# Token-major queries and keys of two chunks by DMA transpose instead of TensorE and ScalarE, in a one-core transformer-layer backward kernel

## The chip, the cores and the metric

The kernel runs on one core of a Trainium2 chip. The metric is the device time of one execution in microseconds; for a kernel it is the median of several runs. The kernel before takes 562.0 us (three runs, 561.25 to 563.71).

## What is computed

One pre-layernorm transformer layer, forward and backward: 2048 tokens of width 512 (D), 32 heads of 16, a sliding and dilated attention (each query sees 8 keys, at distances 0, 2, ... 14), then a GELU feed-forward of width 1792. The outputs are the layer's result and the gradients of the input, of the four weight matrices and of the two biases. Everything is bf16.

```python
def _A_ref(x, wqkv, wo):
    qkv = (x @ wqkv).reshape(B, S, 3, H, Dh)...      # q, k, v per head
    idx = pos[:, None] - (arange(8) * 2)[None, :]    # 8 dilated keys, masked below 0
    logits = einsum("bhsd,bhswd->bhsw", q, k[idx]) * Dh ** -0.5
    o = einsum("bhsw,bhswd->bhsd", softmax(logits), v[idx])
    return o.reshape(B, S, D) @ wo
def _B_ref(x, w1, b1, w2, b2):
    return gelu(x @ w1 + b1) @ w2 + b2
h  = x + _A_ref(layernorm(x), wqkv, wo)
h2 = h + _B_ref(layernorm(h), w1, b1, w2, b2)        # and jax.vjp of all of it with grad_out
```

## The kernel before

**Stages.** The tokens are cut into four chunks (c = 0 to 3) of 512. Per chunk there is an attention forward (`p1_ln`, `p1_qkv`, `p1_attn`, `p1_o`, `p1_h`), the feed-forward with its backward (`p2_h`, `p2_out`, `p2_dg`, `p2_bwd`), and the attention backward (`p3_go`, `p3_dots`, `p3_bands`, `p3_gl1`). At the end come the weight gradients (`wg_ffn`). These are not run one after another: the whole program is a list of about 2000 small operations (`op(...)`), each with an engine, and two tables written out at the end of the file say in which order they are emitted (`ORDER`) and at which SBUF address or PSUM bank each buffer lies (`HOMES`). Every engine works through its own share of that order and stops at the first operation whose inputs or whose buffer are not ready. So an operation that stalls on an engine holds up all that stands behind it there, the DMA issues of SyncE (SP) and of GpSimd (POOL) included.

**Projections.** `p1_proj` multiplies the layernormed chunk by the q or k columns of `wqk` (line 570) and ScalarE evicts the result to `qt` or `kt`, feature-major: features on the partitions, tokens along the row. `kt` has 16 more columns in front (`PAD`), the last tokens of the chunk before; `p1_qkv` copies them from that chunk's `kt` (line 602). `dots` multiplies on VectorE (DVE) four times per chunk: query block times the eight shifted key blocks, one product `prf` of 128 x 4096 (line 428), and TensorE sums it over the features of a head (line 436) with a matrix of ones and zeros, `Emat` or `S32`.

**Token-major copies.** The backward's `gather` reads queries, keys and values back from DRAM token by token (`q_d`, `k_d`, `v_d`), with the features in the order "position in the head, then head". `to_tm_store` makes that copy for q and k: per chunk and tensor two groups of eight 128 x 128 transposes on TensorE (line 393), in which the matrix `Pmat` also reorders the features, one ScalarE eviction per group (line 276, tiles `tmq`, `tmk`) and one store of 256 KB per group on the SP queue (line 266).

**The other way, already in the file.** `tm_dma` does the same by DMA transposes issued from SP (`xload`, line 270) into a tile `tm..d`, and one store of 512 KB. It can't reorder features. In the kernel before only the attention output gradient (`go`, all chunks, tile `tmgod`) goes this way. `TMD` lists who does. `QKP` lists the chunks whose q and k are projected with `wqp`, a copy of `wqk` with its columns already in "position, head" order; it is empty before, and then neither `wqp` nor the copies that fill it exist.

**GpSimd.** POOL computes the layernorm's rstd for chunks 1 to 3 (line 343), issues the gathers (line 418), and makes one reordered weight copy, `woT` from `woR` (line 1066), of the same form and size as each of the two copies that would fill `wqp`.

Of the kernel before, what the change touches and what calls it, by code (L numbers as in the profile page):

```python
# [10 lines left out]
P = 128  # L11
# [9 lines left out]
PAD = 16  # L21
# [127 lines left out]
def kernel(  # L149
# [26 lines left out]
    S, D = xf.shape  # L176
    F = B_w1.shape[1]
    NT = S // P
    CH = 512
# [413 lines left out]
    def p1_qkv(c):  # L593
# [5 lines left out]
        else:  # L599
            kp = st_[c - 1]["kt"]  # L600
            if (c in QKP) == (c - 1 in QKP):
                op("DVE", 0.12, lambda: V.tensor_copy(out=kt()[:, :, 0:PAD], in_=kp()[:, :, CH:CH + PAD]), r=[(kp, 0), (kp, 1)], w=[(kt, "h")], tag="halo")
            else:
                ps = ps_("psh")
                lp = st_[c - 1]["ln1T"]

                def hm():
                    for g in range(4):
                        for dc in range(DC):
                            T.matmul(ps()[:, g * PAD:(g + 1) * PAD], lhsT=wqp()[:, dc, D + g * P:D + (g + 1) * P], rhs=lp()[:, dc, CH - PAD:CH],  # L610
                                     start=(dc == 0), stop=(dc == DC - 1))
                op("PE", 1.0, hm, r=[(wqp, 1), lp], w=[ps], tag="khalo", cls=0)
                op("DVE", 0.15, lambda: V.tensor_copy(out=kt()[:, :, 0:PAD], in_=ps()[:, 0:4 * PAD].rearrange("p (g n) -> p g n", g=4)), r=[ps], w=[(kt, "h")], tag="halo")
# [509 lines left out]
QKP = ()  # L1123
TMD = (('go', 0), ('go', 1), ('go', 2), ('go', 3))
# [162 lines left out]
```

## Time and profile before

| | before |
|---|---|
| median of 3 runs | 562.0 us (561.25 to 563.71) |
| profiled execution, its own time | 562.08 us |
| its span, first to last instruction | 560.3 us |
| TensorE (PE) busy | 538.7 us (96%) |
| VectorE (DVE) busy | 496.2 us (89%) |
| ScalarE (ACT) busy | 314.8 us (56%) |
| mean granted TensorE clock | 0.999 |

The profile is one execution. Busy is the time in which an engine had an instruction running; a matmul's end is modelled, so a busy PE is not yet a PE at its peak. "PEld" is the load of the stationary operand, which overlaps the matmuls. The DMA share is the mean busy share of the core's 16 DMA engines. An idle gap is put down to what ended it. Tiles are shown without their numbers, and a line can be that of a helper: line 276 is every plain eviction, line 270 every DMA transpose.

### The profile page before, as it was taken

The page shows a single profiled execution, that of the slowest core. Times are in us where ns is not written, and L with a number is a line of the kernel's source. Part 1 is how long each engine was busy: PE and PEld are TensorE (multiplying, and loading weights), DVE is VectorE, ACT ScalarE, POOL GpSimd, SP SyncE. Part 2 cuts the span into 40 slices and gives each one's busy share as a digit, 9 for nine tenths or more (in the row PEclk, how much of TensorE's full clock was granted, in tenths as well). Part 3 has the DMA queues.
Part 4 walks back from the last instruction along what each step waited for, and adds up shares of the span by engine and source line. Part 5 has one row for each costly group of instructions (what it writes and reads, how often), then busy time and mean ns, then how long its engine had stood idle before and what let it go on. Part 6 is the DMA issues. An engine that isn't in the chain of part 4 may idle for free. (4 is left out here: it accounts for less than half of the span.)

```text
span 560.3 us, 8579 instructions
## 1 busy us (share of the span) xinstructions
PE 538.7 (96%) x3281; PEld 247.9 (44%) x3330; DVE 496.2 (89%) x651; ACT 314.8 (56%) x498; POOL 36.2 (6%) x55
## 2 busy tenths in 40 slices
PE   7799989999999999999999999999999999999996
PEld 3344444344444444444444444464444444444442
DVE  7989999999999999899886287798999898999944
ACT  4887589997989965885411224222235526543432
POOL 0210011020000100002000000000010110100000
PEclk9999999999999999999999999999999999999999
DMA  8898979999297383479789999999989999887773
GB/s 248 230 286 241 324 247 308 271 236 259 90 242 202 121 188 84 123 151 256 157 151 186 199 207 152 251 211 232 242 272 322 364 274 364 320 332 180 230 190 96
DMA packets 199673, 126.65 MB, mean 226 GB/s; under 512 B 152080, under 2 KB 193232, under 8 KB 195536
## 3 DMA queue, kind: packets, MB, share of 16 engines
q1 hardware_dynamic: 194016, 84.68, 64.3%
q0 software_dynamic: 5616, 41.42, 19.8%
q8 instruction: 26, 0.43, 0.3%
q14 instruction: 15, 0.12, 0.1%
HBM read 55.74 MB, written 35.21 MB: 162 GB/s over the span
## 5 line engine op out<-in xcount | busy, mean ns | idle before, releaser
L276 ACT CAST wgs<-ps 128x512 bf16<-128x512 f32 (+1 forms) x30 | 16.3, 557 | 69.4 <-PE ps L940 61.2
L794 PE MATMUL ps<-goT,w2T 128*128 128x512 bf16 x224 | 54.3, 379 | 0.5 <-DVE h2s L768 0.5
L712 PE MATMUL ps<-ln2T,w 128*128 128x512 bf16 x224 | 53.3, 379 | 0.1
L808 PE MATMUL ps<-w1T,xb 128*128 128x512 bf16 x218 | 51.5, 379 | 0.4
L766 PE MATMUL ps<-w,gl 128*128 128x512 bf16 x219 | 51.2, 379 | 0.6 <-DVE h2s L768 0.3
L714 ACT ACTIVATE xb<-ps,b1c 128x512 bf16<-128x512 f32 x56 | 36.4, 691 | 19.3 <-PE ps L712 19.2
L914 PE MATMUL ps<-wqkvT,gqkvT 128*128 128x512 bf16 x183 | 44.3, 379 | 0.5 <-issue 0.2
L796 DVE SCALAR_TENSOR_TENSOR xb<-xb,ps 128x512 bf16<-128x512 bf16 x56 | 36.7, 681 | 8.7 <-PE ps L794 8.2
L428 DVE TENSOR_TENSOR prb<-got,vw 128x4096 bf16<-128x4096 bf16 x16 | 36.1, 2285 | 8.2 <-ACT got L276 7.0
L940 PE MATMUL ps<-gw1in,ln 128*128 128x512 bf16 (+1 forms) x185 | 38.6, 351 | 0.8 <-issue 0.6
L940 PE MATMUL ps<-gor,gw2in 128*128 128x512 bf16 x164 | 38.8, 379 | 0.2
L467 DVE TENSOR_TENSOR prbv<-Rv,cfv 128x4096 bf16<-128x4096 bf16 x16 | 35.7, 2284 | 2.0 <-DMA Rv<-go_d 1.7
L467 DVE TENSOR_TENSOR prbk<-Rk,cfk 128x4096 bf16<-128x4096 bf16 x16 | 35.9, 2286 | 1.4 <-PE ps L476 1.3
L467 DVE TENSOR_TENSOR prbq<-Rq,cfq 128x4096 bf16<-128x4096 bf16 x16 | 35.9, 2285 | 1.3 <-DMA Rq<-k_d 1.0
L467 DVE TENSOR_TENSOR prbo<-Ro,cfo 128x4096 bf16<-128x4096 bf16 x16 | 35.7, 2281 | 0.0
L428 DVE TENSOR_TENSOR prf<-qt,kt 128x4096 bf16<-128x4096 bf16 x16 | 35.7, 2285 | 0.0
L940 PEld LDWEIGHTS <-ln 128*128 128x128 bf16 x256 | 24.3, 98 | 24.4 <-issue 3.0
L794 PEld LDWEIGHTS <-w2T 128*128 128x128 bf16 x224 | 21.8, 98 | 27.2 <-issue 1.6
L766 PEld LDWEIGHTS <-gl 128*128 128x128 bf16 x224 | 21.7, 98 | 27.2 <-issue 1.1
L808 PEld LDWEIGHTS <-xb 128*128 128x128 bf16 x224 | 21.9, 98 | 26.4
L712 PEld LDWEIGHTS <-w 128*128 128x128 bf16 x224 | 21.3, 98 | 26.2 <-issue 2.1
L570 PE MATMUL ps<-ln1T,wqk 128*128 128x512 bf16 x127 | 30.2, 379 | 2.0 <-DMA wqk<-in_A_wqkv_dram 1.9
(173 smaller groups left out, 964.7 us busy)
## 6 DMA issues: line engine op xcount, KB each, us to landing
Ro<-v_d POOLq DMA_DIRECT2D x4, 1280.0 KB, 9.0
Rq<-k_d POOLq DMA_DIRECT2D x4, 1280.0 KB, 8.5
Rv<-go_d POOLq DMA_DIRECT2D x4, 1280.0 KB, 8.7
Rk<-q_d POOLq DMA_DIRECT2D x4, 1280.0 KB, 6.6
g_d<-gl SPq DMA_DIRECT2D x9, 512.0 KB, 3.8
gh_d<-xb SPq DMA_DIRECT2D x9, 512.0 KB, 3.4
Ro<-v_d POOLq DMA_DIRECT2D x4, 1024.0 KB, 6.3
Rq<-k_d POOLq DMA_DIRECT2D x4, 1024.0 KB, 9.8
```

What stands on the lines that cost most here:

```text
L276: fn = lambda: A.copy(out=ap(), in_=pap())
L428: op("DVE", tt_us(4096), lambda g=g, pr=pr: V.tensor_tensor(out=pr(), in0=ql()[:, g, :].unsqueeze(1).to_broadcast([P, W, 512]), in1=_sub(k ...
L467: V.tensor_tensor(out=pr().rearrange("p a j (d h) -> p a j d h", h=H), in0=_sub(R()[:, o0, 0:1], [[st, 2], [512, 4], [32, DH], [1, H]]), i ...
L570: T.matmul(ps()[:, gg * 512:(gg + 1) * 512], lhsT=wq_()[:, dc, sel * D + g * P:sel * D + (g + 1) * P], rhs=cols(st_[c]["ln1T"], dc, c in F ...
L712: T.matmul(ps(), lhsT=w1()[:, dc, f * P:(f + 1) * P], rhs=cols(ln2T[c], dc, c in FM2), start=(dc == 0), stop=(dc == DC - 1))
L714: op("ACT", act_us(512, 1), lambda f=f, ps=ps, xb=xb, f0=f0: A.activation(out=xb()[:, f - f0, :], in_=ps(), func=ACT.Identity, bias=b1c[:, ...
L766: T.matmul(ps(), lhsT=d["g"][f // 4]()[:, f % 4, j * P:(j + 1) * P], rhs=w2()[:, f, :], start=(f == 0), stop=(f == FT - 1))
L794: T.matmul(ps(), lhsT=w2T()[:, dc, f * P:(f + 1) * P], rhs=cols(goT, dc, True), start=(dc == 0), stop=(dc == DC - 1))
L796: op("DVE", 0.61, lambda f=f, ps=ps, z=z, f0=f0: V.scalar_tensor_tensor(out=z()[:, f - f0, :], in0=z()[:, f - f0, :], scalar=1.0, in1=ps() ...
L808: T.matmul(ps(), lhsT=d["d"][f // 4]()[:, f % 4, j * P:(j + 1) * P], rhs=w1T()[:, f, :], start=(f == 0), stop=(f == FT - 1))
L914: T.matmul(ps(), lhsT=gT()[:, j, b * P:(b + 1) * P], rhs=wqkvT()[:, k0 + b, :], start=(i == 0 and b == 0), stop=(i == 2 and b == 3))
L940: T.matmul(ps()[:, 0:N], lhsT=l, rhs=r, start=(n == 0), stop=(n == k - 1))
```

## The change

`QKP` becomes (2, 3): the queries and keys of chunks 2 and 3 are projected with `wqp`. `TMD` gets q and k of chunks 2 and 3: their token-major copies go through `tm_dma`. What follows from these two settings in code that stands in the file already:

- POOL fills `wqp` in two copies (keys, then queries), each of 2048 elements per partition, from `wqk`. In the new order both stand on POOL behind the rstd of chunk 2 and ahead of that of chunk 3 and of the first gathers of `Ro`.
- Chunk 2's `kt` can't take its 16 front columns from chunk 1's `kt`, whose features lie in another order. They are computed again from chunk 1's `ln1T`: 16 matmuls of 16 columns (`khalo`) and a small DVE copy. The one changed line of code gives the right slice of `ln1T` where that tile is laid out by the DMA transpose (`FM1`).
- `dots` sums the products of chunks 2 and 3 with `S32` instead of `Emat`, in matmuls of the same shape.
- For each of the four (tensor, chunk) pairs, 16 TensorE transposes, two evictions and two stores go; for a query chunk one DMA transpose of 512 KB and a store in 256-byte pieces come, for a key chunk four DMA transposes of 128 KB and a store.

`ORDER` and `HOMES` are new throughout (1982 operations instead of 1989, 869 buffers instead of 879).

```diff
                         for dc in range(DC):
-                            T.matmul(ps()[:, g * PAD:(g + 1) * PAD], lhsT=wqp()[:, dc, D + g * P:D + (g + 1) * P], rhs=lp()[:, dc, CH - PAD:CH],
+                            T.matmul(ps()[:, g * PAD:(g + 1) * PAD], lhsT=wqp()[:, dc, D + g * P:D + (g + 1) * P], rhs=lp()[:, TPC - 1, (dc + 1) * P - PAD:(dc + 1) * P] if c - 1 in FM1 else lp()[:, dc, CH - PAD:CH],
                                      start=(dc == 0), stop=(dc == DC - 1))
...
-QKP = ()
-TMD = (('go', 0), ('go', 1), ('go', 2), ('go', 3))
+QKP = (2, 3)
+TMD = (('go', 0), ('go', 1), ('go', 2), ('go', 3), ('q', 2), ('k', 2), ('q', 3), ('k', 3))
...
 ORDER = (
-    9, 6, 12, 7, 19, 0, 4, 21, 22, 1, 70, 3, 25, 37, 5, 8, 18, 10, 20, 11, 2, 51, 47, 52,
...
```

The code that the settings switch on:

```python
for i in (1, 0) if QKP else ():
    op("POOL", 3.9, lambda i=i: G.tensor_copy(out=wqp()[:, :, i * D:(i + 1) * D].rearrange("p a (d h) -> p a d h", h=H),
                                              in_=_sub(wqk()[:, 0, 0:1], [[2 * D, DC], [1, DH], [DH, H]], i * D)), r=[(wqk, i)], w=[(wqp, i)], tag="hinwq")
...
def tm_dma(fm, off, dst, c, back, tag, pm):
    st = sb("tm" + tag + "d", [P, 4, 512])
    r = c * CH + (RPAD if back else 0)
    if off:
        for g in range(4):
            xload(st, lambda g=g: st()[:, :, g * P:(g + 1) * P], lambda g=g: fm()[:, g, off:off + CH], 128, r=[(fm, g // 2)], key=g, tag="tmx" + tag)
        store(dst, lambda: dst()[r:r + CH, :].rearrange("(a p) d -> p a d", p=P), st, lambda: st(), 512, key=(c, 0), tag="tmst" + tag)
    else:
        xload(st, ..., lambda: fm().rearrange("p g t -> p (g t)"), 512, r=[(fm, 0), (fm, 1)], tag="tmx" + tag)
        store(dst, ..., row=0.25)
```

239 rows, old and new, of tables (HOMES, ORDER) are left out of this document.

## The prediction

> **What bounds the kernel now.** I read the busy totals first, then the table of twenty-microsecond stretches, then who waited for whom inside the stretch that the change touches.
>
> ```profile
> span 560.3 us, 8579 instructions
> PE 538.7 (96%) x3281; PEld 247.9 (44%) x3330; DVE 496.2 (89%) x651; ACT 314.8 (56%) x498; POOL 36.2 (6%) x55
> ...
> 20.00:40.00 20.00, 18.18 (x136) 8.92 (x136) 17.97 (x25) 18.01 (x22) 2.75 (x4) 1.00 0.90 256
> 40.00:60.00 20.00, 19.45 (x145) 8.74 (x146) 20.00 (x10) 14.43 (x20) 0.00 (x0) 1.00 0.85 242
> 60.00:80.00 20.00, 18.96 (x165) 9.84 (x165) 19.86 (x27) 13.50 (x16) 3.04 (x4) 1.00 0.82 297
> 80.00:100.00 20.00, 18.17 (x155) 8.57 (x156) 20.00 (x12) 19.48 (x31) 1.61 (x3) 1.00 0.97 298
> 100.00:120.00 20.00, 19.73 (x128) 8.28 (x128) 19.79 (x32) 19.93 (x24) 1.76 (x2) 1.00 0.94 248
> 120.00:140.00 20.00, 20.00 (x94) 9.00 (x93) 19.39 (x35) 15.59 (x22) 2.15 (x3) 1.00 0.95 252
> 140.00:160.00 20.00, 20.00 (x122) 8.89 (x121) 19.80 (x22) 19.54 (x27) 0.54 (x1) 1.00 0.54 121
> ```
>
> The columns of the stretches are PE, PEld, DVE, ACT and POOL busy, the granted clock, the DMA share and GB/s. Over the whole span PE is the bound: 538.7 of 560.3 us. But the change sits in the attention forward, roughly 20 to 120 us, and there the reading is another. From 40 to 120 DVE is idle for 0.35 us in all (0 + 0.14 + 0 + 0.21), PE for 3.7 (0.55 + 1.04 + 1.83 + 0.27). In that stage VectorE leads and TensorE follows; from 120 on PE is full and has work queued. Who ended the idle time says the same. PE's waits, 20 to 120:
>
> ```profile
> PE ps L393 <- ACT tmv L276: 1.2, 1, 1.2
> PE ps L634 <- DVE mx L629: 1.1, 3, 0.6
> PE ps L436 <- DVE prf L428: 1.1, 1, 1.1
> PE ps L476 <- ACT tmv L276: 0.7, 1, 0.7
> PE ps L393 <- ACT kt L276: 0.2, 1, 0.2
> ```
>
> and DVE's, 20 to 140:
>
> ```profile
> DVE rtr L1053 <- POOL rstd L343: 1.1, 1, 1.1
> DVE r L647 <- PE ps L642: 0.6, 1, 0.6
> DVE h2s L768 <- PE ps L766: 0.4, 1, 0.4
> ```
>
> So two prices matter: what PE and ACT are spared, and what DVE is charged. A microsecond lost on DVE before about 120 us delays the products that PE then sums; a microsecond saved on PE there counts only as far as PE, not DVE, was late.
>
> **What TensorE and ScalarE are spared.**
>
> ```profile
> L393 PE MATMUL ps<-Pmat,qt 128*128 128x128 bf16 x64 | 4.9, 219 | 2.7 <-ACT qt L276 1.6 <-ACT tmv L276 1.2
> L393 PE MATMUL ps<-Pmat,kt 128*128 128x128 bf16 x64 | 4.9, 219 | 0.2 <-ACT kt L276 0.2
> L276 ACT COPY tmk<-ps 128x1024 bf16<-128x1024 bf16 x8 | 8.2, 1024 | 1.1 <-PE ps L393 1.1
> L276 ACT COPY tmq<-ps 128x1024 bf16<-128x1024 bf16 x8 | 8.1, 1029 | 0.1
> ...
> 38.40 0.61 PE L393 MATMUL ps<-Pmat,kt 128*128 128x128 bf16 x8
> 38.85 1.89 PE L570 MATMUL ps<-ln1T,wqk 128*128 128x512 bf16 x8
> ```
>
> Half of the 128 transposes go: 8 groups of 8. A group's pitch is what it delays the next matmul by, 38.85 - 38.40 = 0.45 us (the mean of 219 ns overlaps), so 8 x 0.45 = 3.6 us of PE. The khalo matmuls come back: 16, each with its own weight load and 16 columns. The nearest row is the transpose, 0.45 / 8 = 0.056 us with its weight load and 128 columns; an eighth of that, 0.007, is the other end, so 0.1 to 0.9 us. I take 0.9, since each has a whole weight load. Net 2.7 us of PE. The summing matmuls keep their shape: nothing. ACT loses 8 evictions of 1.03, 8.2 us, in a stage where it is 97 to 100% busy from 80 to 120; PE's waits for ACT above (1.2 + 0.7 + 0.2 = 2.1 us) could shrink.
>
> What is it worth to the end? At most 2.7 + 2.1 = 4.8 us, at least nothing, since PE may spend it waiting for DVE. The new order uses the freed slots for feed-forward matmuls, but these hang on DVE's layernorm statistics too. I take 1.3 us, half of the net PE time: DVE has only 0.35 us of idle time to give up in this stage, yet some of the matmuls that move up don't wait for it.
>
> **What VectorE is charged.** The costly addition is not the transposes but the two POOL copies that fill `wqp`. The trace has their twin, `woT`:
>
> ```profile
> L1066 POOL COPY woT<-woR 128x2048 bf16<-128x2048 bf16 x1 | 3.9, 3888 | 69.6 <-DMA gh_d<-xb 69.6
> ...
> 255.27 3.89 POOL L1066 COPY woT<-woR 128x2048 bf16<-128x2048 bf16 x1 [69.63 <-DMA gh_d<-xb]
> ...
> 134.59 0.69 DVE L733 TENSOR_SCALAR ga<-x 128x2048 bf16<-128x2048 bf16 x1
> ...
> 255.62 4.09 DVE L733 TENSOR_SCALAR ga<-x 128x2048 bf16<-128x2048 bf16 x1
> ...
> 17.38 2.28 DVE L428 TENSOR_TENSOR prf<-qt,kt 128x4096 bf16<-128x4096 bf16 x1
> ...
> 17.47 3.06 POOL L343 TENSOR_TENSOR rstd<-ve,mhalf 128x4 f32<-128x4 f32 x1 [0.76 <-DVE nm L346]
> 31.39 1.01 POOL L343 TENSOR_TENSOR rstd<-ve,mhalf 128x4 f32<-128x4 f32 x1 [10.86 <-DVE ve L341]
> ```
>
> Two readings. At 255.27 the copy starts on POOL, and the DVE instruction that starts at 255.62 takes 4.09 us instead of 0.69: it ends at 259.71, which is the copy's end at 259.16 plus about its own length. DVE stood still while POOL copied. The other way round, POOL's rstd, 1.01 us alone, took 3.06 when it started 0.09 us after a product: it ended 0.87 us after the product did. So DVE and POOL exclude each other here, and the one that came first is not interrupted. The Trainium skill states this as a rule, in SBUF — State Buffer, section "Who interferes with whom": VectorE and GpSimd share a pair of ports, whichever issues first holds it for the whole instruction, and an instruction with two SBUF inputs, as a product is, contends with a GpSimd instruction that reads SBUF. Both rows agree; by that rule alone the copies could also be the ones that wait, which is the first rival.
>
> Where do the copies fall? Ahead of them on POOL stand only the rstd of chunks 1 and 2, and their input `wqk` is in use by the first projections. So they start right behind the rstd of chunk 2, beside the first chunk's four products.
>
> ```profile
> 21.94 4.48 DVE L428 TENSOR_TENSOR prf<-qt,kt 128x4096 bf16<-128x4096 bf16 x2
> ...
> 32.43 0.21 DVE L1053 STREAM_TRANSPOSE rtr<-rstd 128x32 f32<-128x32 f32 x1 [1.12 <-POOL rstd L343]
> ```
>
> In the new order the rstd of chunk 2 is released behind the first product, so it runs when the second ends, near 22 us, and the first copy asks for SBUF during the third product. It gets in behind that, since a small DVE instruction (nm of chunk 2) stands between the third and the fourth, and the fourth then waits 3.9 us less some 0.1. The second copy finds the fourth product waiting or running, lets it pass, and runs in the stretch after it that has no products: from 26.42 (the end of the row above) to 32.43 DVE does statistics and a maximum, 6.0 us without a product, more than the 3.9 needed. So one copy is charged, 3.8 us, with 0 and 7.8 (2 x 3.89) as ends; a gain is excluded, since copies only add. Behind the copies on POOL wait the rstd of chunk 3 and the first gathers. DVE's wait for that rstd, 1.12 us at 32.43, goes: the new order puts the instructions that need it behind the softmax of chunk 0. And the gathers have all four products of chunk 1 for cover, as the new order puts these ahead of the first band product. DVE's net loss is 3.8 - 1.1 = 2.7 us.
>
> **What SP and the DMA engines are charged.**
>
> ```profile
> q_d<-tmq SPq DMA_DIRECT2D x8, 256.0 KB, 3.3
> k_d<-tmk SPq DMA_DIRECT2D x8, 256.0 KB, 3.8
> go_d<-tmgod SPq DMA_DIRECT2D x4, 512.0 KB, 4.4
> tmgod<-got SPq DMA_TRANSPOSE x4, 4.5
> ...
> L270 SPq DMA_TRANSPOSE tmgod<-got x4: 1866/2914/3837, 327.3 to 453.3; - x4
> ...
> 109.46 3.65 SPq L270 DMA_TRANSPOSE w2T<-in_B_w_dram  x2
> ...
> 126.62 1.03 PE L794 MATMUL ps<-goT,w2T 128*128 128x512 bf16 x4
> ```
>
> The stores carry the same bytes in half as many pieces: about nothing. The transposes of 4 x 512 KB are new. One holds the SP queue for 2.9 us at the median, so 4 x 2.9 = 11.7 us of queue, and I take the same for the DMA engines. By their place in the new order they run between about 55 and 150 us. From 60 to 140 the DMA share leaves 20 x (0.18 + 0.03 + 0.06 + 0.05) = 6.4 us, and the next stretch 9.2 more. Nobody needs the copies before the backward's gathers. What stands behind them on SP is wanted, but early: the last of `w2T` was issued by 113.1, landed some 4.5 us later, and was first used at 126.62, 9 us of slack. So I put this at nothing; what it costs if that cover is gone is the third rival.
>
> **Sum.** 562.08 (the profiled execution, its span plus 1.8; the median of the runs is 562.0, so no shift) - 1.3 + 2.7 = 563.5 us. About 0.5%, 2.8 us, is what a measurement of this kernel can tell from no change; this sum lies inside it.
>
> **Rivals.** First, the copies cost DVE nothing: they come late enough, or lose every race, as the rstd did at 17.47. Then PE's relief shows: 562.1 - 2.7 - 1.1 (the wait that goes), 558.3, and down to 556.2 if ACT's 2.1 go too. For it: an order that was planned with such stalls would put the copies where DVE does statistics. Against it: nothing holds POOL until then. Second, slower: both copies go ahead of a product. The second follows the first on POOL at once, before the blocked product is through: 7.8 - 1.1 - 1.3, 567.5 us. It decides where POOL keeps the port between two of its instructions; no row shows that. Third, slower as well, the transposes crowd the DMA: of their 11.7 us 5.3 don't fit before 140, and if the order has put so much of it ahead of `w2T` that this slips beyond its 9 us, PE waits: 563.5 + 5.3 = 568.8. Against it: 9 us is more than 5.3. The Trainium skill speaks for it, in VectorE: DVE Perf Modes, section "The three transpose paths": a 128 x 128 transpose is given as 390 ns on TensorE and 1309 by DMA, and the advice is TensorE where PSUM will do. By an estimate from that page 64 tiles would take 59 us more. The trace agrees in direction only: 0.056 us on PE, 4.5 / 16 = 0.28 by DMA.
>
> **How the numbers follow.** My forecast has 0.42, and its own range is 561 to 566; of it 0.36 lies within 0.5% of before (559.2 to 564.8) and 0.06 above. The first rival has 0.30: 0.24 below 559.2, 0.06 within. The second has 0.18 and the third 0.10, of which 0.26 lie above 564.8 and 0.02 within. Faster 0.24, same 0.44, slower 0.32. The range 557 to 570 leaves out some 0.08 below (ACT's whole relief) and 0.10 above (two slow cases together). As all of the order is new, each case also carries its luck, some microseconds either way.
>
> **What would show it.** One product of chunk 0 of about 6 us instead of 2.28, beside a POOL copy at 22 to 30 us; the other copy beside statistics. PE's idle time from 40 to 120 grown from 3.7 us to 5 or 6, ended by DVE, and none by ACT's `tmv`. DMA share from 80 to 160 higher, with no PE wait on DMA. PE busy 536 in total. I am wrong if all products last 2.28 (first rival), two are long (second), or a wait on `w2T` or `ln2T` appears (third); and if these hold but the time doesn't, the order past 160 us did it.

## The result and the profile after

The changed kernel took 566.9 us, median of 4 runs (566.01 to 567.8), against 561.9 of the kernel before (561.25 to 563.71, 4 runs): a ratio of 1.0084, 95% interval 1.0055 to 1.0112. It is slower by 0.84%. That lies inside the forecast range of 557 to 570, but above the 563.5 that was forecast, above that forecast's own range of 561 to 566, and outside the likeliest class, no change. The number of the prediction that comes nearest is the second rival's 567.5; its mechanism is not what the profiled execution shows. That execution took 566.01 us, the fastest of the four.

The page after, its span and its busy totals; then the stretches of twenty microseconds, with the columns of before:

```profile
span 564.2 us, 8539 instructions
...
PE 542.3 (96%) x3282; PEld 245.0 (43%) x3282; DVE 499.0 (88%) x651; ACT 308.1 (55%) x490; POOL 47.5 (8%) x57
```
```profile
20.00:40.00 20.00, 16.23 (x141) 8.13 (x139) 18.02 (x24) 16.02 (x20) 14.79 (x6) 0.91 0.67 177
40.00:60.00 20.00, 19.23 (x133) 7.24 (x130) 20.00 (x11) 12.28 (x15) 0.00 (x0) 1.00 1.07 303
60.00:80.00 20.00, 18.10 (x139) 8.69 (x139) 19.86 (x27) 11.15 (x14) 2.68 (x4) 1.00 0.94 296
80.00:100.00 20.00, 17.84 (x141) 7.68 (x139) 20.00 (x13) 15.47 (x25) 1.59 (x3) 1.00 0.87 251
100.00:120.00 20.00, 18.50 (x128) 8.24 (x126) 19.83 (x27) 19.39 (x23) 1.61 (x2) 1.00 1.15 279
120.00:140.00 20.00, 19.93 (x94) 8.92 (x92) 19.86 (x38) 17.80 (x24) 1.03 (x1) 1.00 0.91 220
140.00:160.00 20.00, 18.08 (x102) 7.86 (x101) 16.62 (x18) 16.15 (x24) 1.48 (x2) 1.00 0.79 255
```

ScalarE's 314.8 us became 308.1: 6.7 of the 8.2 us that the eight evictions were put at. TensorE's total can't be compared: the trace of before holds 3330 weight loads but 3281 matmuls, so 49 records of matmuls are missing there. The first stretch has what matters: TensorE 16.2 us busy instead of 18.2 and a granted clock of 0.91. And a later stretch that was full before, 140 to 160, now has VectorE idle for 3.4 us and TensorE for 1.9.

VectorE's timeline in the first stretch (start, duration), and POOL's:

```profile
20.53 2.28 DVE L428 TENSOR_TENSOR prf<-qt,kt 128x4096 bf16<-128x4096 bf16 x1
22.73 3.88 DVE L346 SCALAR_TENSOR_TENSOR nm<-mv,rstd 128x4 f32<-128x4 f32 x1
26.53 2.28 DVE L428 TENSOR_TENSOR prf<-qt,kt 128x4096 bf16<-128x4096 bf16 x1
28.73 0.68 DVE L330 BATCH_NORM_STATS2 st<-xt 128x6 f32<-128x512 bf16 x1
...
36.54 0.69 DVE L649 TENSOR_TENSOR attn<-e,r 128x1024 bf16<-128x1024 bf16 x1
```
```profile
21.36 11.21 POOL L1010 COPY wqp<-wqk 128x2048 bf16<-128x2048 bf16 x2
```

The copies asked for SBUF at 21.36, the third product held it until 22.73, then the first copy ran; it was the tiny `nm` (128 x 4) that stood still, 3.88 us instead of 0.15, with the fourth product queued behind it. The second copy lost to that product and ran beside the statistics, which kept their 0.68 us. TensorE, in the same place, and its clock in two stretches of 2 us:

```profile
28.86 1.04 PE L436 MATMUL ps<-prf,Emat 128*32 128x512 bf16 x8 [3.76 <-DVE prf L428]
29.84 2.94 PE L570 MATMUL ps<-ln1T,wqk 128*128 128x512 bf16 x8
```
```profile
28.00:30.00 2.00, 1.14 (x9) 0.26 (x9) 1.64 (x4) 2.00 (x4) 2.00 (x1) 0.64 0.86 293
30.00:32.00 2.00, 2.00 (x6) 0.66 (x5) 1.97 (x3) 1.81 (x3) 2.00 (x1) 0.51 0.11 37
```

It waited 3.76 us for the product and came back at about half its clock: eight projection matmuls took 2.94 us, where the same eight take 1.89 a little later.

The difference can be cut into legs with four marks that every trace has: the start of the first product (`prf`), the start of the first attention instruction (`attn<-e,r`), the end of the last band product (`prbo`), and the end of the last matmul. In us, each from the mark before:

| kernel | first product | to attention | to last band product | to last matmul |
|---|---|---|---|---|
| before | 17.38 | 16.96 | 118.53 | 402.55 |
| after | 15.97 | 20.57 | 124.02 | 398.21 |

The last two columns belong together, since the new order moves work across the mark: 521.08 before, 522.23 after. So the change of 3.9 us in span (560.3 to 564.2) is -1.41 before the first product, +3.61 from there to attention, +1.15 from attention to the last matmul, and +0.55 in the tail behind it.

### The profile page after: what moved, and what is told of

The parts are those of the page before. It is cut to its first block, busy times and chain, and to the rows that moved or that the text cites. A ratio compares the mean times of both kernels' runs of the same rounds, so it can differ in the third digit from the quotient of the medians.

```text
span 564.2 us, 8539 instructions
## 1 busy us (share of the span) xinstructions
PE 542.3 (96%) x3282; PEld 245.0 (43%) x3282; DVE 499.0 (88%) x651; ACT 308.1 (55%) x490; POOL 47.5 (8%) x57
## 3 DMA queue, kind: packets, MB, share of 16 engines
q1 hardware_dynamic: 205536, 86.78, 66.5%
## 4 chain that ended last, share of the span: by engine, by line
PE 75%; DVE 16%; DMA 3%; ACT 3%; issue 2%; SPq 0%; POOL 0%; DVEq 0%; POOLq 0%; ACTq 0%
PE ps L940 27%; PE ps L808 9%; PE ps L914 7%; PE ps L794 7%; PE ps L766 6%; DVE prf L428 5%; PE ps L476 4%; PE ps L712 2%; PE ps L832 2%; PE ps L570 2%; DVE prbo L467 2%; PE ps L436 2%; DVE st L330 2%; DMA xp<-in_A_x_dram 1%; PE ps L492 1%
## 5 line engine op out<-in xcount | busy, mean ns | idle before, releaser
L712 PE MATMUL ps<-ln2T,w 128*128 128x512 bf16 x224 | 52.0, 379 | 1.5 <-DMA ln2T<-ln 1.4
L940 PE MATMUL ps<-gor,gw2in 128*128 128x512 bf16 x168 | 40.0, 379 | 0.0
L940 PE MATMUL ps<-gw1in,ln 128*128 128x512 bf16 (+1 forms) x192 | 40.0, 353 | 0.0
L736 ACT ACTIVATE xb<-xb 128x2048 bf16<-128x2048 bf16 (+1 forms) x16 | 26.8, 1688 | 5.0 <-DVE xb L735 5.0
```

What stands on the lines that cost most here:

```text
L712: T.matmul(ps(), lhsT=w1()[:, dc, f * P:(f + 1) * P], rhs=cols(ln2T[c], dc, c in FM2), start=(dc == 0), stop=(dc == DC - 1))
L736: op("ACT", act_us(N), lambda xb=xb: A.activation(out=fl(xb), in_=fl(xb), func=ACT.Tanh, scale=GC), w=[xb], tag="tanh", mode=6)
L940: T.matmul(ps()[:, 0:N], lhsT=l, rhs=r, start=(n == 0), stop=(n == k - 1))
```

## Experiments

Beside these runs the kernel before took 562.4 to 563.6 us at the median; the ratios with their intervals come from the runs of both kernels, and so differ a little from those of the medians. Legs of the profiled executions, by the same marks (the first leg holds the arrival of the first weights, for which TensorE waits up to 4.2 us, differently in each execution):

| run | first product | to attention | to last band product | to last matmul | median us, ratio with interval |
|---|---|---|---|---|---|
| e4, before + copies | 16.90 | 26.17 | 118.53 | 403.08 | 571.2, 1.0142 (1.0108 to 1.0176) |
| e8, before relieved | 17.01 | 16.97 | 118.92 | 402.86 | 562.2, 0.9968 (0.9946 to 0.9991) |
| e1, copies on ACT | 15.96 | 21.19 | 124.10 | 398.72 | 567.5, 1.0084 (1.0055 to 1.0113) |
| e2, no transposes | 16.94 | 20.50 | 124.70 | 398.43 | 568.2, 1.0095 (1.0066 to 1.0124) |
| e3, e1 and e2 | 15.99 | 20.78 | 124.90 | 398.34 | 567.8, 1.0111 (1.0063 to 1.0158) |
| e5, no copies | 18.34 | 17.07 | 128.47 | 398.70 | 569.4, 1.0101 (1.0057 to 1.0144) |
| e6, gather early | 18.41 | 24.82 | 122.81 | 399.11 | 571.7, 1.0133 (1.0094 to 1.0172) |
| e7, e5 and e6 | 16.66 | 17.02 | 128.05 | 398.85 | 568.6, 1.0084 (1.0056 to 1.0112) |
| e9, as after | 15.57 | 25.23 | 124.00 | 398.77 | 570.9, 1.0142 (1.0118 to 1.0166) |
| e10, e9 and gather early | 15.79 | 19.60 | 122.35 | 398.59 | 565.4, 1.0069 (1.0041 to 1.0098) |
| e11, copies held | 16.48 | 18.31 | 124.48 | 398.64 | 563.8, 1.0029 (1.0002 to 1.0056) |
| e12, e11 and gather early | 16.02 | 18.29 | 122.33 | 398.62 | 565.2, 1.0026 (1.0007 to 1.0046) |

The last leg is the same to within 0.9 us in all runs with the new order. What VectorE loses ahead of the last band product is lost at the end.

**e1, e2, e3: each suspect alone, then both.** The copies go to ScalarE; or the ten DMA transposes are left out.

```diff
-        op("POOL", 3.9, lambda i=i: G.tensor_copy(out=wqp()...
+        op("ACT", 1.8, lambda i=i: A.copy(out=wqp()...      # keys' copy ahead of the first exp
```
```diff
-            xload(st, ..., tag="tmx" + tag)                  # all ten
-            store(dst, ..., st, ...)
+            store(dst, ..., wo, ...)                         # as many bytes, from another tile
```

> The changed kernel, with the two copies that fill wqp on ScalarE instead of POOL (queries right behind the first chunk's ln1T eviction, keys ahead of the first exp); all else and the order of everything else as in the changed kernel. Theory 1, the port: the changed kernel's nm instruction of 3.88 us, PE's wait of 3.76 us behind it and the clock's dip after it (0.64 and 0.51 from 28 to 32 us) come from the POOL copy. Then all products and nm are at their normal length, PE clock stays at 1.00 from 20 to 40, and the time falls by 3.8 + 1.5 less some 1.0 for ACT's own 3.6 us: about 562 to 563. Theory 2, crowded DMA from 80 to 160 us (the Ro wait of 2.1 us, the ln2T wait of 1.4): the early stall is absorbed before that, so the time stays within 1.5 us of 566.9. Theory 3, the order's luck: the same, about 566.

> The changed kernel without the ten DMA transposes of queries and keys of chunks 2 and 3 (left out: those transposes; the four stores write wo's contents instead, in the same pieces, so the gradients of these tokens are not the reference's). Theory 1, the port: the stall at 22 to 30 us stays, so at most 1 to 2 us are won: 565 to 566. Theory 2, crowded DMA: the waits for Ro and ln2T on DVE and PE (2.1 and 1.4 us) go, PE's idle time from 80 to 160 falls by about 3.5 us, time about 563. Theory 3, the order's luck: unchanged, 566 to 567.

> Copies on ScalarE and the ten DMA transposes left out together (the stores write wo's contents, so the gradients of these tokens are not the reference's). If port and DMA are two separate charges, their gains add: about 559 to 560, which is also what the spared TensorE work alone should give (562 - 2.7). If only one matters, it equals the better of the two single runs. If it is the order's luck, it stays near 566.

e1 took 567.5, e2 568.2, e3 567.8: none gained. A stretch of e2, with the columns of above:

```profile
60.00:80.00 20.00, 18.00 (x135) 8.53 (x136) 19.86 (x28) 11.15 (x13) 2.68 (x4) 1.00 0.68 230
```

The DMA share fell from 0.94 to 0.68, and the leg in which the transposes lie did not shrink (124.70 against 124.02): they cost nothing that shows. In e1 and e3, without the POOL copies, `nm` took 0.15 us and the fourth product 2.28, so VectorE's stall is the copies'. The time of e1 settles nothing, as it exchanged that stall for another. ScalarE's timeline and TensorE's longest wait, 20 to 42 us:

```profile
28.70 3.89 ACT L1010 COPY wqp<-wqk 128x2048 bf16<-128x2048 bf16 x1
32.61 1.28 ACT L637 ACT_TABLE_LOAD   x1
```
```profile
PE ps L642 <- ACT e L637: 4.9, 1, 4.9
```

The copy that was put at 1.8 us took 3.89, and the exponential behind it came late by that.

**e4: the two POOL copies alone, in the kernel before,** right behind the rstd of chunk 2, into a buffer that nobody reads.

```diff
-    for i in (1, 0) if QKP else ():
+    for i in (1, 0):
-    wqp = sb("wqp", [P, DC, 2 * D]) if QKP else None
+    wqp = sb("wqp", [P, DC, 2 * D])
```

> The kernel before, unchanged but for the two POOL copies, put on POOL right behind the rstd of chunk 2 and written to a buffer that nobody reads. Theory 1, the port: the first copy stops the DVE instruction behind the second product for 3.9 us; the last two products stand back to back here, so the second copy either waits for both (one stop, about 567 with the clock's dip) or gets in between them (two stops, 570 to 572). Theories 2 and 3: the copies hide, 562 to 563.

571.2 us against 562.4 of the kernel before in the same runs: two instructions whose result nobody reads, on an idle engine, cost 8.7 us. VectorE's timeline, where `x2` is two products in one row, POOL's, and the row of all four products:

```profile
21.39 3.86 DVE L346 SCALAR_TENSOR_TENSOR nm<-mv,rstd 128x4 f32<-128x4 f32 x1
25.17 8.17 DVE L428 TENSOR_TENSOR prf<-qt,kt 128x4096 bf16<-128x4096 bf16 x2
...
20.01 11.18 POOL L1010 COPY wqp<-wqk 128x2048 bf16<-128x2048 bf16 x2
...
L428 DVE TENSOR_TENSOR prf<-qt,kt x4: 2280/2284/5970, 16.9 to 27.4; 128x4096 bf16<-128x4096 bf16 x4
```

Here both copies stopped something: `nm` lost 3.7 us to the first, and the two products took 8.17 instead of 4.48 (their row in the profile before). The third product still went ahead of the second copy, as the 11.18 us for both copies show; the fourth stands right behind the third here, so the copy got in ahead of it, and it took 5.97. TensorE's clock was 0.50 from 30 to 38 us.

**e8: the relief alone, in the kernel before.** The eight groups of transposes and the eight evictions are left out.

```diff
         for j2 in range(TPC // 2):
+            if tag in "qk" and c > 1:
+                tm_store2(wo, ...)       # the same store, from another tile
+                continue
             pt = ps_("ptm" + tag)
```

> Kernel before with its order, and nothing of the change but the relief: the eight groups of TensorE transposes and the eight ScalarE evictions of the queries and keys of chunks 2 and 3 are left out, and the eight stores write other bytes of the same count (so what the backward gathers there is not the queries and keys). It measures the term of 1.3 us that the prediction took for the relief: 560.7 if that is right, 557.3 if all of TensorE's 3.6 and ScalarE's waits were on the path, 562 if VectorE sets the end of this stage and nothing of it is worth anything.

562.2 us, a ratio of 0.9968. In the profiled executions nothing moved: every leg agrees with before to 0.4 us, and the execution took 562.38 against 562.08. The runs of before that it is compared with were spread more than usual (561.4 to 566.0), and the fastest of both are equal (561.3 and 561.4). So the relief is worth between nothing and 0.5%; the trace puts it at nothing, as it should where VectorE, not TensorE, is late.

**e5, e6, e7: no copies at all, and the late gather.** In e5 the buffer is filled by two more loads of unpermuted weights. e6 takes up a second loss: in the stretch 140 to 160 VectorE waited for the gather of the last chunk's value rows. The rows of the profile after, on VectorE and POOL:

```profile
150.81 2.29 DVE L467 TENSOR_TENSOR prbo<-Ro,cfo 128x4096 bf16<-128x4096 bf16 x1 [2.11 <-DMA Ro<-v_d]
```
```profile
140.85 1.48 POOL L418 DMA_DIRECT2D Ro<-v_d  x2 [12.84 <-DVE xb L735]
```

Before, it was issued at 123.34. In the new assignment of homes its buffer lies over two gelu buffers, and the issue waited for VectorE to free them. e6 gives those two other homes and puts the gather behind the last rstd.

```diff
-        op("POOL", 3.9, lambda i=i: G.tensor_copy(out=wqp()...
+        load(wqp, lambda i=i: wqp()[:, :, i * D:(i + 1) * D], ..., 512, key=i, tag="hinwq")
```
```diff
 # e6, in ORDER: both halves of chunk 3's gather, from positions 568 and 593 to 513
 # e6, in HOMES: x2 of block 0: 2773 -> 224; ga of block 2: 2709 -> 1409
```

> Kernel after, but the two POOL copies that permute the weights are left out: the buffer is filled by two more loads of 512 KB on SP at the same place of the order, with the weights not permuted (so the queries and keys of chunks 2 and 3 have their channels in the old order, and the group sums under them are of the wrong channels); everything else, order and homes too, is that of after. Theory A (the port conflict is what was lost): the 3.88 us nm goes back to 0.15, the 3.76 us wait of TensorE for the third product goes, the granted clock of 20 to 40 us is 1.00 again, the attention instruction that starts at 36.54 starts 4 to 5 us earlier, and the kernel takes 562 us. Theory B (the new order loses its time later): the stretch 20 to 40 heals in the same way, but VectorE and TensorE then meet the same late buffers at 140 us and the same small waits, and the kernel takes 564.5 to 566.5. The two loads cost some 3 us of SP queue and, by either theory, nothing else.

> Kernel after, but the gather of the last chunk's value rows (the two issues at 140.85) stands in POOL's order right behind the last rstd, as in the kernel before; to make room the homes of two gelu buffers (x2 of block 0 and ga of block 2 of the second half) are others, so that its home is free by then. Theory A: those 2.1 us of VectorE and the TensorE wait behind it lie where TensorE has its backlog, so nothing: 566.5. Theory B: the gather lands near 138 instead of 150.8, VectorE's 2.11 us wait goes, TensorE's waits for products at 150 to 160 (3.2 us) shrink by 2, and the kernel takes 564.5 to 565.

> Both of the edits before: no POOL copies (two unpermuted loads instead) and the early gather. Theory A: as without copies, 562. Theory B: the sum of the two, 4 to 5 of the stall and 2 of the gather, 560 to 560.5; if the stall is hidden by a later wait, removing both gives more than the two alone.

569.4, 571.7 and 568.6: all three missed by both theories, and each for a reason that its own trace shows. Without copies the way to attention is 17.07 and 17.02 us, so their price in the profile after is 20.57 - 17.05 = 3.5 us. But the two loads gave it back: in e7 the transpose behind them held SP for 6.02 us instead of 1.91 (in after, at 31.41; 2.77 and 2.98 in e1 and e3, which have neither the POOL copies nor the loads), and TensorE waited for what it brings. SP's and TensorE's timelines of e7:

```profile
30.22 6.02 SPq L270 DMA_TRANSPOSE ln1T<-ln  x1
...
133.20 5.46 SPq L270 DMA_TRANSPOSE tmkd<-kt  x1
...
141.45 3.05 SPq L270 DMA_TRANSPOSE ln2T<-ln  x1
```
```profile
38.37 1.69 PE L588 MATMUL ps<-wv,ln1T 128*128 128x512 bf16 x4 [4.12 <-DMA ln1T<-ln]
...
146.06 1.89 PE L712 MATMUL ps<-ln2T,w 128*128 128x512 bf16 x8 [2.36 <-DMA ln2T<-ln]
```

The last rows are what the early gather cost: with it in flight, a transpose of keys held SP for 5.46 us, and the `ln2T` queued behind it came 2.36 us late. And in e6 the fourth product took 6.00 us, TensorE waited 6.7 us in one piece, and the way to attention was 24.8 us, with POOL's and VectorE's instructions there those of after. In the profiled executions of e5 and e6 the first product also starts 2.4 us later than in after, as the first weights came late (TensorE waits 2.0 and 4.2 us for them, 0.6 in after).

**e9: the race.** The copies were to be held until the fourth product is done.

```diff
-    ... r=[(wqk, i)], w=[(wqp, i)], tag="hinwq")
+    ... r=[(wqk, i), pr3], w=[(wqp, i)], tag="hinwq")    # pr3: the fourth product's buffer
```

> Kernel after with its order and homes, but the two POOL copies are held until the fourth product of chunk 0 is done (they read that product's buffer too), so that they run beside statistics and the maximum instead of ahead of a product. All of the computation is there. Theory A (the port conflict is what was lost): nm takes 0.15 us instead of 3.88, the fourth product starts near 23 and ends near 25, the copies run from 25 to 33, TensorE's 3.76 us wait and the lower granted clock behind it go, the first attention instruction starts near 33 instead of 36.54, and the lead of 3.5 us is kept to the end: 562 to 562.5. Theory B (later waits take the place of what goes): the same up to 40 us, and the lead is eaten up between 80 and 165 us by late transposes of ln2T and the late gather of the last chunk: 564.5 to 566. A third possibility, that statistics are held by the copies as products are, would show as DVE instructions of several us beside them, and 566.5.

570.9 us, and the edit did nothing of the kind: the list of reads is only the planner's, no operand changed, and on every engine the instructions stand in the same sequence as in after. So it is after once more, with another outcome. VectorE's and POOL's timelines:

```profile
22.32 3.89 DVE L346 SCALAR_TENSOR_TENSOR nm<-mv,rstd 128x4 f32<-128x4 f32 x1
26.14 6.00 DVE L430 TENSOR_TENSOR prf<-qt,kt 128x4096 bf16<-128x4096 bf16 x1
```
```profile
20.96 9.04 POOL L1033 COPY wqp<-wqk 128x2048 bf16<-128x2048 bf16 x2
```

This time the second copy followed the first at once (9.04 us for both, not 11.21) and the fourth product took 6.00. TensorE waited 7.88 us and ran at a clock of 0.50 from 28 to 36. That is 4.7 us more on the way to attention than in after. With the same instructions in the same sequence, what is left is who comes first at one moment; what decides it, no trace shows.

**e10: e9, and the gather repaired.** The gather as in e6, and two transposes of keys behind the last `ln2T`.

```diff
 # ORDER: chunk 3's gather behind pow2@6; tmxk@4#0 and #2 behind fmln2@6
```

> As e9, and besides: the gather of the last chunk's value rows stands right behind the last rstd (two gelu buffers have other homes for that), and the two transposes of the last chunk's keys that SP issued at 128.46 and 130.69 stand behind the last transpose of ln2T, so that they can't hold it up while the gather is in flight (in the run with both edits before, the second of them held SP from 133.20 for 5.46 us and the ln2T behind it came 2.36 us late for TensorE). All of the computation is there. Theory A: what lies past 120 us has TensorE's backlog for cover, so it is as e9 to within 0.5. Theory B: the gather lands near 135, no wait on Ro or ln2T is left past 120 us, and the time is 2 us below e9; if both hold, near 560, below the kernel before.

Ten runs: seven from 563.6 to 566.1 and three from 569.9 to 570.3, two groups some 5 us apart on average, which is the size of the race. The profiled execution is of the first group; no trace shows the three. Their mean granted clock, 0.988 to 0.990, is that of e9's four runs (0.988 and 0.989), and that of the seven, 0.993 to 0.998, is near that of after's (0.994 to 0.997). In the profiled execution the leg to the last band product is 122.35, 1.7 below after. TensorE waited as long as in after, and its clock stayed at 1.00:

```profile
28.71 0.61 PE L440 MATMUL ps<-prf,Emat 128*32 128x512 bf16 x8 [3.79 <-DVE prf L430]
29.26 1.90 PE L574 MATMUL ps<-ln1T,wqk 128*128 128x512 bf16 x8
```

The way to attention is 19.60 us, 0.97 shorter than in after (and 0.90 shorter than in e2, whose clock dipped too), with VectorE's and POOL's instructions there as long as in after: the clock alone.

**e11, e12: the copies really held.** POOL first copies one column of the fourth product, which it can't do before that is there.

```diff
+            op("POOL", 0.1, lambda: G.tensor_copy(out=wqp()[:, 0, 0:1], in_=pr3()[:, 0, 0:1]), ..., tag="hold")
             for i in (1, 0):
                 op("POOL", 3.9, lambda i=i: G.tensor_copy(out=wqp()...
```

> Kernel after with its order and homes, and one more instruction: ahead of the two copies POOL copies one column of the fourth product of chunk 0 into the buffer that they fill, so that they can't start before that product is done (in e9 they were only planned to read it, read nothing of it, and still started at 20.96). All of the computation is there. Theory A (the port conflict is what was lost): nm takes 0.15 us, the fourth product runs from about 23 to 25, the copies from 25 to 33 beside statistics and the maximum, TensorE's wait of 3.8 us (7.9 in e9) goes, attention starts near 33 instead of 36.54, and of after's 566.9 some 3.5 to 4.5 us go: 562.5 to 563.5, and no run is 4 us above the others, since no race is left for the second copy to win. Theory B (the lead is lost later, at the late gather and ln2T): the same up to 40 us, and 565 to 566.5. If the copies hold statistics too, or attention's product at 33: 566 or more.

> As e11, and besides the edits of e10 (the last chunk's gather right behind the last rstd, two transposes of keys behind the last ln2T). All of the computation is there. Theory A: both losses are separate, so 2 us below e11: 560.5 to 561.5, faster than before by 0.2 to 0.4%. Theory B: it is the gather's edit alone that pays, and this is as e10's faster runs, 564 to 565.

e11 took 563.8 us. By its ratio that is 1.6 us above the kernel before, where the change had cost 4.7: 3.1 us are gone. POOL's and VectorE's timelines of e11:

```profile
25.73 0.19 POOL L1033 COPY wqp<-prf 128x1 bf16<-128x1 bf16 x1 [3.82 <-DVE prf L430]
25.98 7.75 POOL L1035 COPY wqp<-wqk 128x2048 bf16<-128x2048 bf16 x2
```
```profile
23.24 0.15 DVE L346 SCALAR_TENSOR_TENSOR nm<-mv,rstd 128x4 f32<-128x4 f32 x1
23.32 2.28 DVE L430 TENSOR_TENSOR prf<-qt,kt 128x4096 bf16<-128x4096 bf16 x1
...
30.18 3.58 DVE L606 COPY kt<-kt 128x64 bf16<-128x64 bf16 x1
33.69 0.16 DVE L341 TENSOR_SCALAR ve<-mv 128x4 f32<-128x4 f32 x1
```

`nm` and the product are free, the clock is 1.00. The second copy now stops another small instruction, the 16 front columns of the next keys, for 3.58 us; some slack lies behind it, and 18.31 - 17.05 = 1.3 us of it reaches attention. "No run 4 us above the others" did not hold: six of the 11 runs lie from 563.4 to 563.8, the other five from 565.1 to 575.9. The trace is of the lowest of the five (565.12), which shows the copies held all the same; what sets the two groups apart stays open. In e12 the gather is issued at 126.07, the leg to the last band product is 2.15 us shorter than in e11, and the profiled execution took 562.48. But its twelve runs spread from 562.0 to 567.5 with a median of 565.2, no better than e11. So the gather's 2 us are shown in the traces, and not in the times. Neither version beats the kernel before.

## Why the prediction came out as it did

**The copies: right step, and a missing half.** One copy blocked, at the predicted place, between the third product and the fourth, for the predicted time (3.88 - 0.15 = 3.73, forecast 3.8), and the other ran beside statistics. The victim was `nm`, not the product; to TensorE that is the same. So all four products lasted 2.28 us, by the letter of the prediction's signs a point for the first rival, which had the copies cost nothing; the 3.88 us of `nm` and the time refute it. With the slack that hides part of it, the stall alone is worth 19.60 - 17.05 = 2.55 us (e10 against e5 and e7).

That the forecast's net loss of 2.7 lies so near is luck: it was 3.8 less the 1.1 us of the wait for rstd. That wait did go, but without copies the way to attention is no shorter for it (17.05 against 16.96 before), since VectorE waits for TensorE's softmax sums instead (2.03 and 1.98 us in e5 and e7, 0.59 before).

What failed is that the working ended at VectorE: TensorE's wait of 3.76 us brought its clock down, and that cost 0.97 us more, together 3.5. By the clock of the 2-us stretches (0.64 and 0.51) TensorE ran at half for some 3.4 us, an estimate. The profile of before has no TensorE wait of that length in this stage, so no row showed it. The Trainium skill does: TensorE: Matmul & The Clock Gate, Part 1, says that the gate halves the clock after a free-running window of about 3.4 us without work. The traces agree in part. The half clock followed waits of 3.76 us (after), 3.78 (e2) and all longer ones, such as the 7.88 of e9 (0.50 from 28 to 36); it did not follow 3.79 in e10, nor 3.46 in e5, which a window that runs freely allows. But it also came without such a wait. TensorE's timeline of e5, and its clock there:

```profile
88.37 1.54 PE L712 MATMUL ps<-ln2T,w 128*128 128x512 bf16 x4 [1.42 <-DMA ln2T<-ln]
...
88.00:90.00 2.00, 1.63 (x5) 0.68 (x6) 2.00 (x2) 0.00 (x1) 0.00 (x0) 0.68 0.74 143
90.00:92.00 2.00, 2.00 (x6) 0.76 (x5) 2.00 (x2) 1.58 (x2) 1.00 (x2) 0.50 1.13 250
```

The longest wait just ahead is 1.42 us. So the length of one wait doesn't decide it, and what does, these runs leave open.

**The second rival was real.** It named the open point, whether POOL keeps the port between two instructions, and gave it 0.18. The answer is that either can happen with the same instructions: by their traces after, e2, e4 and e10 on the side where a product got in between the copies, e6 and e9 on the other, and by time and clock three runs of e10 with them. The forecast of 7.8 us for two copies compares with 25.23 - 17.05 = 8.2 in e9, again with the clock. By their times the four runs of after all fell on the cheaper side, which is luck. So is it that their 566.9 lies beside the rival's 567.5: one copy was charged, not two, and the clock, the late gather and the relief that didn't come made up the rest.

**The relief: mis-sized.** Of the 2.7 us of TensorE time 1.3 were put to the end. e8 shows 0 in its legs, and its times allow some 0.5% at most. In the new order it is no more: with the gather repaired, attention to last matmul takes 520.94 (e10) and 520.95 (e12), against 521.08 before. The bound "at least nothing" was the right end, and the argument for it stood in the text: VectorE had only 0.35 us to give up. The `khalo` matmuls were taken at 0.9 us and took 0.40, inside the 0.1 to 0.9 that were given. The timeline of after, whose starts give the pitch:

```profile
39.57 0.55 PE L610 MATMUL ps<-ln1T,wqp 128*128 128x16 bf16 x16
39.97 1.02 PE L570 MATMUL ps<-ln1T,wqk 128*128 128x512 bf16 x4
```

**The transposes: right.** They were put at nothing, and e2 finds nothing. The third rival fell, since leaving them out gains nothing. The profile pages give the DMA time: the hardware queues' packets took 66.5% of 16 engines' span in after and 63.6% in e2, so the ten transposes took some 15 us of all 16 engines, an estimate, where 11.7 were forecast; other work hid them. The estimate of some 59 us more for the 64 tiles from the Trainium skill, VectorE: DVE Perf Modes, section "The three transpose paths", is not borne out in the time. A wait on `ln2T` of 1.4 us did appear in after, one of the signs of the third rival, but it stays at 1.2 without the ten transposes, so it is the order's.

**The order: named and not priced.** "Some microseconds either way" was all that was said. Ahead of the first product these two executions differ by 1.4 us, but part of that is the arrival of the first weights: where TensorE waits 0.6 to 0.7 us for them, the first product starts at 15.57 to 16.02 in the new order (e9, after, e12) and at 16.90 in the old (e4), so the order gave some 0.9 to 1.3. It took about 2 at the late gather. That was to be found at 140 to 160 us, not past 160.

The terms as measured: -1.4 (first leg) + 3.6 (copies 3.5 and 0.1 else) + 1.15 (late gather 1.7 to 2.2, less what the rest of the order gave) + 0.55 (tail) = 3.9. Of the signs foretold, TensorE's idle time from 40 to 120 grew from 3.7 to 6.3 us, half of it ended by VectorE; the waits for `tmv` fell from 1.9 to 0.3, and the DMA share from 80 to 160 rose from 0.85 to 0.93. The 536 us of TensorE can't be judged, for the missing records. The longest of TensorE's waits, 40 to 120, in after:

```profile
PE ps L476 <- DVE prbo L467: 1.6, 3, 0.9
PE ps L712 <- DMA ln2T<-ln: 1.4, 1, 1.4
PE ps L436 <- DVE prf L428: 1.0, 4, 0.3
```

## What to carry to other kernels

Before giving an idle POOL a long SBUF instruction, list what VectorE runs for as long as it lasts, the tiny instructions too: a two-input instruction of 4 columns and a copy of 64 columns stood still as long as a product would, while statistics and maxima from PSUM did not. If two such POOL instructions stand in a row, count both as charged unless an operand forces them past the products; the same program went either way, 4 to 5 us apart. And follow a stall on to TensorE: a wait of 3.8 us may also cost clock there, 0.97 us here.

## What the runs showed of the hardware

- A POOL copy of 128 x 2048 that reads with a stride takes 3.89 us, and so does ScalarE's (3.90): moving it buys nothing but the port.
- Which DVE instructions wait for POOL's reads: `nm` with two SBUF inputs (3.88 us instead of 0.15), the product (6.00 instead of 2.28), a bf16 copy of 64 columns (3.58 instead of 0.15). Statistics (0.68), the maximum over PSUM (1.23) and the mask on PSUM (0.29) kept their times. The Trainium skill draws the same line in SBUF — State Buffer, section "Who interferes with whom": two SBUF inputs, or a mode of copies that uses both ports.
- Two POOL copies in a row may or may not let a waiting VectorE instruction in between: with the same instruction sequence the second took 6.05 us behind a product of 2.28 in after, and 3.85 in e9, where the product took 6.00.
- A DMA transpose on SP's queue behind large plain transfers can hold the queue: 6.02 and 5.46 us behind two loads of 512 KB (e7, e5) instead of 1.91 in after and 2.77 to 2.98 in e1 and e3, and 5.1 to 5.6 with the gather in flight (e6, e7, e10, e12). What stands behind it pays.
- TensorE's clock after 3.8 us of idle time was 0.51 in one execution and 1.00 in another: 0.97 us on the way to attention. In e5 it fell to 0.50 with no wait above 1.42 us just ahead.
